# First weights loaded four pieces ahead, second weights split by VectorE and ScalarE, in an attention and two-MLP kernel

## The chip, the cores and the metric

The kernel runs on one core of one Trainium2 chip. The metric is the device time of one execution in microseconds. Before the change it is 1040.72 us, the median of 3 runs (1040.44 to 1042.83).

## What is computed

Three stages, each fed by the one before: a block-causal attention over 4 batches of 8 heads, 576 positions and 64 columns a head; an MLP with leaky ReLU; and a second MLP with a piecewise activation. The reference, cut:

```python
mask = (pos[:, None] // 64) >= (pos[None, :] // 64)
attn = softmax(np.where(mask, q @ k.T / np.sqrt(D), -1e9)) @ v     # per batch and head
x = attn.transpose(0, 2, 1, 3).reshape(2304, 512)
h = x @ w_in                       # 512 -> 2048, first MLP
x = np.maximum(0.01 * h, h) @ w_out
h = x @ w2_in                      # second MLP
g = np.where(h >= 1, h, np.where(h <= -1, 0.0, (h + 1) ** 2 / 4))
out = g @ w2_out
```

## The kernel before, in words

Products need more precision than one pass gives, so most operands are split into a high and a low part ("hi" and "lo", made by a copy and a subtraction) and three products are added up on TensorE (`three`, L536 to L539). The first batch's attention runs in plain float32 instead.

**Weights.** Both MLPs' weights come in as 64-bit words and lie in 16 slices f of 2 pieces each, 32 pieces an MLP, 512 KB a piece. `load_w1` (L127) issues the load of a piece on SyncE's queue. `convert_w1` makes float32 of it in four instructions: a scale on ScalarE or PoolE (L43, L47), then L113, L114 and L115 on VectorE. After the second piece of a slice, `split_w` makes hi and lo of its two halves: `w1i` for the up-projection and `w1o` for the down-projection. All these tiles share one pool of 33 slots. `w_to(n)` converts up to piece n, and `load_to` runs ahead of it by `WL` pieces; `WL` pieces are also loaded before anything else but the first two heads:

```python
loads_to(1)                            # L616, L617
load_to(C["WL"])
...
while nw < min(n, 2 * KF):             # w_to, L607 to L611
    load_to(nw + C["WL"])
    with behind(C["pW"]):
        convert_w1(nw)
    nw += 1
```

In the first batch's attention one piece is converted every seven items, up to twelve; the rest is converted in block 0 of the first MLP, two pieces for each f.

**Heads.** `load_head` issues queries (L236), keys (L237) and values (L251) of a head of the first batch, or L241, L247 and L255 of a later one. The tiles have two slots, so head 2 can be loaded when head 0's scores are done.

**Order.** Tokens of the first MLP come in 9 blocks of 256. Everything up to block 6 is traced and then put in order by a planner (`arrange`): it simulates the five engines with costs of its own, takes on each engine the earliest traced instruction that is ready by its model, and fixes each engine's order, SyncE's queue of transfers among them. An engine then runs in that order, and waits where an operand or a buffer is not there yet. A tile gets its slot only after the first user of the tile before it in the same pool has started, so the place of a load in the trace limits how early it can be issued. From block 6 on the planner has no part.

**Second weights.** In blocks 6 and 7 `stage_w2` converts them and writes them to DRAM (`wdram`), through three buffers (load L148, store L151). In block 8, as each f of the first weights is used up, `split_w2` loads a slice back (L155) and splits it with the same `split_w`:

```python
copy(nc, pick(he, 2 * f + u, ph), x[:, 0], w[:, u])
tt(nc, pick(le, 2 * f + u, ph), x[:, 1], w[:, u], f32(x)[:, 0], ALU.subtract)
```

Here u is 0 for `w2i` and 1 for `w2o`, and `pick` takes the letter at that place: D is VectorE, A ScalarE, P PoolE. A copy shows as L30 on ScalarE and L32 on VectorE; a subtraction is L38 on either VectorE or PoolE. In the same stretch VectorE makes gh (L32, for every second f) and gl (L38) of the first MLP.

**Second MLP.** 5 blocks, four of 512 tokens and one of 256. `up2` clamps (L718), squares on ScalarE (L719), takes the maximum (L720) and splits (L721, L722); `down2` adds up output tiles of 128 tokens, m = 0 to 3, copies each from PSUM by `copy(nc, pick("osE", m), osb, ot[m])` (L738) into one of three buffers, and stores it from ScalarE's queue (L739).

Of the kernel before, what the change touches and what calls it, by code (L numbers as in the profile page):

```python
# [14 lines left out]
ALU = mybir.AluOpType  # L15
AX = mybir.AxisListType

C = {'yx': 2, 'WARM': 7, 'DT': [0, 0, 1, 1], 'LAGD': 2, 'VLD': 4, 'WS': 1, 'RS': 2, 'zb': 2, 'dhE': 'PA', 'dlE': 'DD', 'wrE': 'SSSA', 'rdE': 'S', 'PR': '', 'pW': '', 'pS': '', 'p2': '', 'pL': '', 'pG': '', 'lkE': 'D', 'fE': 'A', 'stF': 'A', 'SPLIT': [0, 0, 0, 0], 'WIN': [[0.75, 1.86], [2, 3.86], [3.9, 5.86]], 'PF': [8, 0, 0, 0], 'VF': [8, 0, 0, 0], 'FL': 2, 'LD': 1, 'rcE': 'D', 'fold': 'D', 'evL': 'D', 'ptb': 1, 'PACE': 1, 'LAG0': 1, 'LAG': 3, 'VL0': 2, 'VL': 1, 'YL': 1, 'YL2': 3, 'gB': 2, 'ghB': 3, 'F32S': 6, 'F32V': 6, 'CS': 4, 'CR': 7, 'CN': 12, 'WAHEAD': 5, 'WL': 10, 'cE': 'APPP', 'addE': 'DP', 'hiE': 'AA', 'loE': 'DD', 'evH': 'AAD', 'xeE': 'A', 'norm': 'PPPPP', 'vhiE': 'D', 'vloE': 'P', 'ghE': 'DA', 'glE': 'DD', 'xhE': 'AAPP', 'xlE': 'PDDP', 'B1S': 0.5, 'FILL': 0.96, 'STR': 1.2, 'sc': 4, 'g': 3, 'gh': 3, 'klE': 'D', 'khE': 'P', 'stA': 'PP', 'stC': 'PA', 'yevE': 'DA', 'w2lo': 'DP', 'w2hi': 'DD', 'S0': 'att', 'T0': 'y', 'V0': 'h', 'natt': 5, 'evA': 'A', 'LY': 4, 'LYB': 4, 'yhE': 'AD', 'ylE': 'DD', 'osE': 'AA', 'qhE': 'D', 'sg': 3, 'TS': 1, 'norm_0': 'P', 'xlE_1': 'DPPP', 'evH_0': 'A', 'xhE_1': 'ADPA', 'norm_1': 'ADADA', 'fold_0': 'P', 'qhE_1': 'D', 'glE_0': 'DD', 'evA_1': 'AA', 'klE_2': 'P', 'klE_3': 'P', 'vloE_3': 'P', 'qhE_2': 'A', 'khE_2': 'P', 'vhiE_1': 'P', 'vloE_2': 'P', 'vloE_1': 'P', 'qhE_3': 'A', 'xlE_2': 'PDDP', 'xeE_2': 'AD', 'vhiE_3': 'A', 'norm_2': 'DADPA', 'xeE_1': 'DA', 'xhE_0': 'DDAA', 'xlE_0': 'PDPP', 'evH_1': 'A', 'evA_0': 'AA', 'fold_1': 'P', 'vloE_0': 'D', 'vhiE_0': 'D', 'khE_1': 'P', 'ghE_1': 'DD', 'fE_e': 'AP', 'hiE_e': 'AA', 'loE_e': 'DD', 'dlE_3': 'PD'}
P = 128
NEG = -1.0e30  # L20
EPS = 1.0e-9
# [29 lines left out]
def attention_moe_moe(ctx: ExitStack, tc: tile.TileContext, qkv, w1, w2, out, B, H, S, D):  # L51
# [22 lines left out]
    ps = [pctx.enter_context(tc.tile_pool(name="ps", bufs=1, space=bass.MemoryType.PSUM))]  # L74
    C["nh"] = 6 - C["natt"]
    nbanks = {"y": 2, "h": C["nh"], "att": C["natt"] - (2 if C["PR"] else 0)}

# [51 lines left out]
    def convert_w1(n):  # L129
        f, u = n // 2, n % 2  # L130
        ph = "e" if n < C["CN"] else ""
        if u == 0:
# [25 lines left out]
    def pick(n, i, ph=None):  # L158
        e = C.get(f"{n}_{ph}") or C.get(f"{n}_{str(ph)[:1]}") or C[n]
        return e[i % len(e)]  # L160
# [4 lines left out]
    two_p = mctx.enter_context(tc.tile_pool(name="two", bufs=2, side="right"))  # L165
    gpool = (two_p, C["g"], C["gh"])
    actx = ExitStack()
# [25 lines left out]

    passes = [(b, gs) for b in range(B) for gs in ([(0,), (1,)] if C["SPLIT"][b] else [(0, 1)])]
    due = [(b * S + GROUPS[gs[0]][0]) // NB for b, gs in passes]
# [812 lines left out]
```

## Time and profile before

| | |
|---|---|
| median of 3 runs | 1040.72 us |
| the profiled execution | 1038.87 us |
| its span, first to last instruction | 1037.1 us |
| TensorE busy | 1000.7 us, 96% |
| VectorE busy | 713.9 us, 69% |
| ScalarE busy | 470.7 us, 45% |
| PoolE busy | 224.8 us, 22% |
| mean granted clock of TensorE | 0.992 |

The rows in a later section come from that one execution. Times are microseconds from the start of its span; PE is TensorE, PEld its weight loads, DVE VectorE, ACT ScalarE, POOL PoolE (GpSimd), SP SyncE, which only issues transfers. A matmul in float32 leaves two records. Busy time is no limit by itself: an engine that waits costs time only where TensorE, the fullest engine, waits for it in the end.

### The profile page before, as it was taken

Reading aid. Unit: us, or ns where it says so; the run is one execution under the profiler, and the core shown is the slowest. Engines: PE = TensorE matmul, PEld = TensorE weight load, DVE = VectorE, ACT = ScalarE, POOL = GpSimd, SP = SyncE. Lnnn points to the kernel's source line nnn. Section 1 sums busy time; section 2 is a strip of 40 time slices with the busy share of each in tenths; the row PEclk is TensorE's granted clock in tenths of the full one; section 3 lists DMA queues with packets and bytes.
Section 4 is the critical chain, followed back from the end, with each engine's and each line's share of the span. In section 5 each row is a group of like instructions: output and inputs, shape, how many; then the busy total and the mean of one; then the engine's idle time right before and its main releaser. Section 6 shows DMA issues by size and latency. Waiting matters only on the chain. (4 is left out here: it accounts for less than half of the span.)

```text
span 1037.1 us, 16659 instructions
## 1 busy us (share of the span) xinstructions
PE 1000.7 (96%) x5518; PEld 847.1 (82%) x5518; DVE 713.9 (69%) x1850; ACT 470.7 (45%) x1167; POOL 224.8 (22%) x291
## 2 busy tenths in 40 slices
PE   8799999999989999999999999999999999999998
PEld 6557888888878888898988797888888888888897
DVE  7889999998898878877787798435334433433343
ACT  6678667675555644554443321223323322322233
POOL 4345022243333454644010144000000000000000
PEclk9999999999999999999999999999999999999999
DMA  9745023227778776774889884001100100000010
GB/s 352 262 152 178 22 51 77 59 64 150 150 139 182 156 150 145 142 169 99 276 298 282 250 273 121 1 1 41 41 1 1 62 1 1 36 5 1 1 41 21
DMA packets 194117, 115.39 MB, mean 111 GB/s; under 512 B 148208, under 2 KB 167152, under 8 KB 194032
## 3 DMA queue, kind: packets, MB, share of 16 engines
q1 hardware_dynamic: 165840, 106.47, 37.3%
q10 hardware_dynamic: 28192, 7.87, 3.2%
q8 instruction: 43, 0.70, 0.3%
q14 instruction: 42, 0.34, 0.1%
HBM read 83.62 MB, written 30.67 MB: 110 GB/s over the span
## 5 line engine op out<-in xcount | busy, mean ns | idle before, releaser
L537 PE MATMUL h<-xh,w1i 128*128 128x256 f32 x576 | 166.9, 290 | 5.8 <-ACT g L542 5.5
L538 PE MATMUL h<-xl,w1i 128*128 128x256 f32 x576 | 164.4, 286 | 1.2 <-DVE xl L38 0.9
L539 PE MATMUL h<-xh,w1i 128*128 128x256 f32 x576 | 164.1, 285 | 0.0
L719 ACT ACTIVATE sq<-cl,half 128x512 f32<-128x512 f32 (+1 forms) x80 | 54.4, 679 | 202.6 <-DVE cl L718 202.6
L718 DVE TENSOR_SCALAR cl<-hh 128x512 f32<-128x512 f32 (+1 forms) x80 | 51.0, 637 | 121.5 <-PE hh L539 121.4
L537 PEld LDWEIGHTS h<-xh,w1i 128*128 128x128 f32 x576 | 109.5, 190 | 15.4 <-ACT g L542 10.3
L567 PE MATMUL y<-w1o,gh 128*128 128x512 f32 x288 | 117.1, 407 | 2.4 <-DVE gh L32 2.1
L300 ACT ACTIVATE p<-s,nm 64x64 f32<-64x64 f32 (+2 forms) x192 | 91.1, 478 | 62.2 <-DVE nm L286 27.0
L537 PE MATMUL hh<-yh,w2i 128*128 128x512 f32 (+1 forms) x320 | 118.1, 369 | 0.3 <-DVE gg L720 0.3
L538 PE MATMUL hh<-yl,w2i 128*128 128x512 f32 (+1 forms) x320 | 118.0, 369 | 0.0
L539 PE MATMUL hh<-yh,w2i 128*128 128x512 f32 (+1 forms) x320 | 117.8, 368 | 0.0
L538 PEld LDWEIGHTS h<-xl,w1i 128*128 128x128 f32 x576 | 109.8, 191 | 5.8 <-DVE xl L38 1.9
L568 PE MATMUL y<-w1o,gh 128*128 128x512 f32 x288 | 114.2, 396 | 0.0
L734 PE MATMUL o<-w2o,ggl 128*128 128x512 f32 x288 | 114.0, 396 | 0.0
L735 PE MATMUL o<-w2o,ggh 128*128 128x512 f32 x288 | 113.9, 395 | 0.0
L539 PEld LDWEIGHTS h<-xh,w1i 128*128 128x128 f32 x576 | 109.8, 191 | 0.6
L570 PE MATMUL y<-w1o,gl 128*128 128x512 f32 x288 | 92.3, 399 | 2.3 <-DVE gl L38 2.2
L720 DVE TENSOR_TENSOR gg<-hh,sq 128x512 f32<-128x512 f32 (+1 forms) x80 | 51.0, 637 | 56.0 <-ACT sq L719 55.8
L286 DVE TENSOR_REDUCE nm<-s 128x1 f32<-128x288 f32 (+2 forms) x192 | 80.0, 424 | 9.3 <-PE s L277 5.6
L47 POOL TENSOR_SCALAR p<-p,rc 128x448 f32<-128x448 f32 (+4 forms) x88 | 60.6, 694 | 119.1 <-ACT p L300 34.9
L733 PE MATMUL o<-w2o,ggh 128*128 128x512 f32 x288 | 86.0, 396 | 0.0
L542 ACT ACTIVATE g<-h 128x256 f32<-128x256 f32 x144 | 54.2, 379 | 69.6 <-PE h L539 58.1
(110 smaller groups left out, 2059.4 us busy)
## 6 DMA issues: line engine op xcount, KB each, us to landing
wr<-in_w_dram SPq DMA_DIRECT2D x64, 512.0 KB, 5.4
wdram<-wt SPq DMA_DIRECT2D x32, 256.0 KB, 3.7
w<-wdram SPq DMA_DIRECT2D x16, 512.0 KB, 5.2
rq<-in_qkv_dram SPq DMA_DIRECT2D x24, 288.0 KB, 3.0
rk<-in_qkv_dram SPq DMA_DIRECT2D x24, 288.0 KB, 2.9
pT1l<-z SPq DMA_DIRECT2D x16, 384.0 KB, 3.9
ydram<-yx SPq DMA_DIRECT2D x72, 64.0 KB, 2.2
out_dram<-osb ACTq DMA_DIRECT2D x18, 256.0 KB, 2.9
```

What stands on the lines that cost most here:

```text
L47: return nc.gpsimd.tensor_scalar(out, in_, by, 1.0, op0=ALU.mult, op1=ALU.mult)
L286: mark["D"] = nc.vector.tensor_reduce(nm[:n, j:j + 1], s[:n, :kw], axis=AX.X, op=ALU.max, negate=True)
L300: mark["A"] = nc.scalar.activation(o, s, AF.Exp, bias=nm[:n, 0:1], scale=es, accum_out=sm[:n, j:j + 1])
L537: nc.tensor.matmul(ps_ap, wh, xh, start=first, stop=False)
L538: nc.tensor.matmul(ps_ap, wh, xl, start=False, stop=False)
L539: nc.tensor.matmul(ps_ap, wl, xh, start=False, stop=last)
L567: nc.tensor.matmul(yt[m], gh[:, ms], wh, start=f == 0, stop=False)
L568: nc.tensor.matmul(yt[m], gh[:, ms], wl, start=False, stop=False)
L570: nc.tensor.matmul(yt[m], gl[:, ms], wh, start=False, stop=f == KF - 1)
L733: nc.tensor.matmul(ot[m], gh[:, ms], wh, start=f == 0, stop=False)
L734: nc.tensor.matmul(ot[m], gl[:, ms], wh, start=False, stop=False)
L735: nc.tensor.matmul(ot[m], gh[:, ms], wl, start=False, stop=f == KF - 1)
```

## The change

Four entries of the table of settings `C` change. `WL` goes from 10 to 4: four pieces of the first weights are loaded at the start, and each later one is loaded four pieces ahead of the conversion in the trace. `w2hi` and `w2lo` give the engines that split the second weights: the high part of `w2i` moves from VectorE to ScalarE, and the low part of `w2o` from PoolE to VectorE; the high part of `w2o` and the low part of `w2i` stay on VectorE. `osE` moves the PSUM copies of output tiles with m = 1 and m = 3 from ScalarE to VectorE.

```diff
 C = {
...
-    'WL': 10,
+    'WL': 4,
...
-    'w2lo': 'DP', 'w2hi': 'DD',
+    'w2lo': 'DD', 'w2hi': 'AD',
...
-    'osE': 'AA',
+    'osE': 'AD',
...
 }
```

## Rows read from the trace of the kernel before

**Rows 1.** Busy time by stretch (us, instructions), granted clock, transfer share, GB/s.
```profile
core 0: us, PE busy (x) PEld busy (x) DVE busy (x) ACT busy (x) POOL busy (x), PEclk, DMA share, GB/s
0.00:95.70 95.70, 82.94 (x378) 56.27 (x378) 83.11 (x312) 69.75 (x207) 41.41 (x60) 0.96 0.67 235
95.70:142.00 46.30, 45.47 (x291) 40.59 (x292) 45.35 (x108) 30.13 (x69) 5.18 (x4) 1.00 0.20 66
142.00:490.00 348.00, 333.81 (x2165) 297.91 (x2164) 300.01 (x933) 205.46 (x594) 144.84 (x203) 0.99 0.59 126
614.60:632.70 18.10, 16.38 (x93) 13.75 (x92) 17.77 (x29) 2.79 (x7) 9.68 (x6) 1.00 0.68 228
```

**Rows 2.** The same view, shorter stretches of the first batch's attention.
```profile
19.00:36.50 17.50, 12.90 (x60) 8.18 (x60) 17.33 (x57) 11.48 (x34) 5.07 (x7) 1.00 1.00 371
40.00:45.00 5.00, 2.38 (x10) 1.56 (x11) 4.91 (x13) 3.04 (x10) 2.80 (x4) 0.99 0.67 224
45.00:50.00 5.00, 5.00 (x24) 3.83 (x22) 2.71 (x9) 2.50 (x6) 1.41 (x2) 0.67 0.37 103
60.00:65.00 5.00, 2.54 (x14) 1.60 (x13) 3.86 (x22) 2.50 (x7) 2.83 (x5) 1.00 0.95 333
65.00:70.00 5.00, 5.00 (x16) 2.35 (x15) 3.92 (x16) 4.39 (x15) 1.51 (x2) 0.66 0.52 199
```

**Rows 3.** TensorE's timeline: start, duration, instruction, in brackets the wait before it.
```profile
4.64 4.37 PE L277 MATMUL s<-kh,qs 128*64 128x64 f32 x12
...
26.48 2.63 PE L277 MATMUL s<-kh,qs 128*64 128x64 f32 x10
...
64.13 0.30 PE L277 MATMUL s<-kh,qs 128*64 128x64 f32 x2 [2.46 <-DMA kh<-in_qkv_dram]
```

**Rows 4.** Timeline of the transfer queue on SyncE: issues, not landings.
```profile
3.55 8.13 SPq L127 DMA_DIRECT2D wr<-in_w_dram  x10
12.80 0.33 SPq L236 DMA_DIRECT2D qs<-in_qkv_dram  x1
14.02 0.33 SPq L237 DMA_DIRECT2D kh<-in_qkv_dram  x1
```

**Rows 5.** Issue to landing, min/median/max: queries (0 to 95 us), first weights (to 140).
```profile
DMA to landing us min/median/max: 3.0/4.5/9.6
...
DMA to landing us min/median/max: 3.5/6.5/11.1
```

**Rows 6.** TensorE's timeline at the end of block 8 and the start of the second MLP.
```profile
628.94 0.50 PE L567 MATMUL y<-w1o,gh 128*128 128x512 f32 x1 [1.09 <-DVE gh L32]
...
632.17 0.73 PE L570 MATMUL y<-w1o,gl 128*128 128x512 f32 x2 [0.63 <-DVE gl L38]
...
644.10 0.50 PE L537 MATMUL hh<-yh,w2i 128*128 128x512 f32 x1 [0.30 <-DVE gg L720]
```

**Rows 7.** Timelines of VectorE and of PoolE in block 8.
```profile
605.13 0.29 DVE L32 CAST gh<-g 128x256 fp32r<-128x256 f32 x1
...
615.89 1.39 DVE L32 CAST gh<-g 128x256 fp32r<-128x256 f32 x1
...
615.51 1.62 POOL L38 TENSOR_TENSOR w2o<-w,w2o 128x512 fp32r<-128x512 f32 x1 [1.69 <-DVE w2o L32]
```

**Rows 8.** Groups of instructions: busy us, mean ns of one, idle time before.
```profile
L718 DVE TENSOR_SCALAR cl<-hh 128x512 f32<-128x512 f32 (+1 forms) x80 | 51.0, 637 | 121.5 <-PE hh L539 121.4
...
L38 DVE TENSOR_TENSOR w2i<-w,w2i 128x512 fp32r<-128x512 f32 x16 | 11.9, 747 | 0.0
...
L30 ACT ACTIVATE w1i<-w 128x512 fp32r<-128x512 f32 x16 | 10.1, 629 | 4.3 <-DVE w L115 4.3
...
L32 DVE CAST w2o<-w 128x512 fp32r<-128x512 f32 x16 | 6.7, 418 | 0.0
```

**Rows 9.** ScalarE's timeline at output copies: a block's fourth, and the last two.
```profile
819.38 0.60 ACT L30 ACTIVATE osb<-o 128x512 f32<-128x512 f32 x1 [2.70 <-DMA out_dram<-osb]
...
1032.85 1.09 ACT L30 ACTIVATE osb<-o 128x512 f32<-128x512 f32 x2 [1.75 <-PE o L735]
```

**Rows 10.** Waits, whole span: us in total, times, longest.
```profile
DVE wr L113 <- DMA wr<-in_w_dram: 12.1, 14, 1.9
```

**Rows 11.** Waits of the transfer queue on SyncE, 0 to 150 us.
```profile
SPq L251 <- PE v L424: 13.5, 2, 7.2
```

More of the change, by code (lines that the diff above doesn't have):

```diff
@@ L16 @@
 AX = mybir.AxisListType
-C = {'yx': 2, 'WARM': 7, 'DT': [0, 0, 1, 1], 'LAGD': 2, 'VLD': 4, 'WS': 1, 'RS': 2, 'zb': 2, 'dhE': 'PA', 'dlE': 'DD', 'wrE': 'SSSA', 'rdE': 'S', 'PR': '', 'pW': '', 'pS': '', 'p2': '', 'pL': '', 'pG': '', 'lkE': 'D', 'fE': 'A', 'stF': 'A', 'SPLIT': [0, 0, 0, 0], 'WIN': [[0.75, 1.86], [2, 3.86], [3.9, 5.86]], 'PF': [8, 0, 0, 0], 'VF': [8, 0, 0, 0], 'FL': 2, 'LD': 1, 'rcE': 'D', 'fold': 'D', 'evL': 'D', 'ptb': 1, 'PACE': 1, 'LAG0': 1, 'LAG': 3, 'VL0': 2, 'VL': 1, 'YL': 1, 'YL2': 3, 'gB': 2, 'ghB': 3, 'F32S': 6, 'F32V': 6, 'CS': 4, 'CR': 7, 'CN': 12, 'WAHEAD': 5, 'WL': 10, 'cE': 'APPP', 'addE': 'DP', 'hiE': 'AA', 'loE': 'DD', 'evH': 'AAD', 'xeE': 'A', 'norm': 'PPPPP', 'vhiE': 'D', 'vloE': 'P', 'ghE': 'DA', 'glE': 'DD', 'xhE': 'AAPP', 'xlE': 'PDDP', 'B1S': 0.5, 'FILL': 0.96, 'STR': 1.2, 'sc': 4, 'g': 3, 'gh': 3, 'klE': 'D', 'khE': 'P', 'stA': 'PP', 'stC': 'PA', 'yevE': 'DA', 'w2lo': 'DP', 'w2hi': 'DD', 'S0': 'att', 'T0': 'y', 'V0': 'h', 'natt': 5, 'evA': 'A', 'LY': 4, 'LYB': 4, 'yhE': 'AD', 'ylE': 'DD', 'osE': 'AA', 'qhE': 'D', 'sg': 3, 'TS': 1, 'norm_0': 'P', 'xlE_1': 'DPPP', 'evH_0': 'A', 'xhE_1': 'ADPA', 'norm_1': 'ADADA', 'fold_0': 'P', 'qhE_1': 'D', 'glE_0': 'DD', 'evA_1': 'AA', 'klE_2': 'P', 'klE_3': 'P', 'vloE_3': 'P', 'qhE_2': 'A', 'khE_2': 'P', 'vhiE_1': 'P', 'vloE_2': 'P', 'vloE_1': 'P', 'qhE_3': 'A', 'xlE_2': 'PDDP', 'xeE_2': 'AD', 'vhiE_3': 'A', 'norm_2': 'DADPA', 'xeE_1': 'DA', 'xhE_0': 'DDAA', 'xlE_0': 'PDPP', 'evH_1': 'A', 'evA_0': 'AA', 'fold_1': 'P', 'vloE_0': 'D', 'vhiE_0': 'D', 'khE_1': 'P', 'ghE_1': 'DD', 'fE_e': 'AP', 'hiE_e': 'AA', 'loE_e': 'DD', 'dlE_3': 'PD'}
@@ new lines @@
+C = {'yx': 2, 'WARM': 7, 'DT': [0, 0, 1, 1], 'LAGD': 2, 'VLD': 4, 'WS': 1, 'RS': 2, 'zb': 2, 'dhE': 'PA', 'dlE': 'DD', 'wrE': 'SSSA', 'rdE': 'S', 'PR': '', 'pW': '', 'pS': '', 'p2': '', 'pL': '', 'pG': '', 'lkE': 'D', 'fE': 'A', 'stF': 'A', 'SPLIT': [0, 0, 0, 0], 'WIN': [[0.75, 1.86], [2, 3.86], [3.9, 5.86]], 'PF': [8, 0, 0, 0], 'VF': [8, 0, 0, 0], 'FL': 2, 'LD': 1, 'rcE': 'D', 'fold': 'D', 'evL': 'D', 'ptb': 1, 'PACE': 1, 'LAG0': 1, 'LAG': 3, 'VL0': 2, 'VL': 1, 'YL': 1, 'YL2': 3, 'gB': 2, 'ghB': 3, 'F32S': 6, 'F32V': 6, 'CS': 4, 'CR': 7, 'CN': 12, 'WAHEAD': 5, 'WL': 4, 'cE': 'APPP', 'addE': 'DP', 'hiE': 'AA', 'loE': 'DD', 'evH': 'AAD', 'xeE': 'A', 'norm': 'PPPPP', 'vhiE': 'D', 'vloE': 'P', 'ghE': 'DA', 'glE': 'DD', 'xhE': 'AAPP', 'xlE': 'PDDP', 'B1S': 0.5, 'FILL': 0.96, 'STR': 1.2, 'sc': 4, 'g': 3, 'gh': 3, 'klE': 'D', 'khE': 'P', 'stA': 'PP', 'stC': 'PA', 'yevE': 'DA', 'w2lo': 'DD', 'w2hi': 'AD', 'S0': 'att', 'T0': 'y', 'V0': 'h', 'natt': 5, 'evA': 'A', 'LY': 4, 'LYB': 4, 'yhE': 'AD', 'ylE': 'DD', 'osE': 'AD', 'qhE': 'D', 'sg': 3, 'TS': 1, 'norm_0': 'P', 'xlE_1': 'DPPP', 'evH_0': 'A', 'xhE_1': 'ADPA', 'norm_1': 'ADADA', 'fold_0': 'P', 'qhE_1': 'D', 'glE_0': 'DD', 'evA_1': 'AA', 'klE_2': 'P', 'klE_3': 'P', 'vloE_3': 'P', 'qhE_2': 'A', 'khE_2': 'P', 'vhiE_1': 'P', 'vloE_2': 'P', 'vloE_1': 'P', 'qhE_3': 'A', 'xlE_2': 'PDDP', 'xeE_2': 'AD', 'vhiE_3': 'A', 'norm_2': 'DADPA', 'xeE_1': 'DA', 'xhE_0': 'DDAA', 'xlE_0': 'PDPP', 'evH_1': 'A', 'evA_0': 'AA', 'fold_1': 'P', 'vloE_0': 'D', 'vhiE_0': 'D', 'khE_1': 'P', 'ghE_1': 'DD', 'fE_e': 'AP', 'hiE_e': 'AA', 'loE_e': 'DD', 'dlE_3': 'PD'}
```

## The prediction

> **What bounds the kernel now.** I read the busy time by stage first, then fine windows where TensorE is not full, then the timelines of TensorE and of the transfer queue around those gaps. The four stretches of [rows 1] show a kernel that TensorE bounds nearly everywhere, with VectorE close behind. In the first 95.70 us, in which the first batch's eight heads run, TensorE is busy 82.94 us and VectorE 83.11 us: neither is full, so the stage is a chain of short waits between engines. In block 0 (95.70 to 142) both are full, 45.47 and 45.35 us of 46.30. From 142 to 490 us TensorE idles 348.00 - 333.81 = 14.2 us in all.
>
> Inside the first stage [rows 2] place the idle time. From 19.00 to 36.50 us TensorE idles 17.50 - 12.90 = 4.6 us while the transfer engines are full (share 1.00, 371 GB/s) and VectorE is busy 17.33 us. From 40 to 45 and from 60 to 65 us it idles 2.62 and 2.46 us. After each of these two the granted clock falls: 0.67 and 0.66 on average over the next 5 us, so part of each runs at 1.2 instead of 2.4 GHz, and loses about 0.33 x 5 = 1.7 us of full-speed time. [Rows 3] name two causes: the first scores of head 2 start only at 26.48 us, and the gap near 64 us ends with a key load (2.46 us).
>
> [Rows 4] say why head 2 is late. The transfer queue issues the ten pieces ahead in 8.13 us from 3.55 us on, so head 2's queries go out at 12.80 and its keys at 14.02 us. [Rows 5]: a query load lands after 3.0 us at best and 9.6 us at worst in this stage, so 12.80 + 9.6 = 22.4 us.
>
> The other place is the end of block 8. Between 614.60 and 632.70 us VectorE is busy 17.77 of 18.10 us and TensorE 16.38 [rows 1]; the waits that end last there are 1.09 us for gh and 0.63 us for gl, and later 0.30 us for gg [rows 6], 2.0 us together, all on VectorE.
>
> **The change part by part.**
>
> *Six pieces fewer at the start.* Six loads of 512 KB leave the head of the queue: 3.15 MB at 371 GB/s [rows 2] are 8.5 us of full transfer engines. Every later piece moves too: all 28 pieces after the first four are now issued some three conversions before their own, behind loads of heads (L236, L237, L251, and L241, L247, L255 for the second batch) that they used to pass. Nothing is added in number. The queries of head 2 need only head 0's scores out of the way, which are over at 4.64 + 4.37 = 9.0 us [rows 3]; so an issue near 9 us and a landing 4.5 us later, the median of [rows 5], gives 14 us in place of 22.4. What that frees on TensorE is at most the 4.6 us of idle time from 19.00 to 36.50 us. VectorE is full there (17.33 of 17.50 us), partly with conversions that fill its time and can slide into later idle, so I take half: 2.3 us. Bounds: 4.6 + 2.46 + 1.7 = 8.8 us if the gap at 64 us and the drop of clock behind it go too, and a loss by late pieces, priced among the rivals. I do not take the key stall itself: in the middle of the stage one piece is loaded per piece converted, before as after, so the same transfers share the engines there. Block 0 covers conversions that slide: VectorE's total to 142 us is 128.5 of 142 us, and TensorE, busy 45.47 of 46.30 us in block 0 [rows 1], hardly waits for the conversions there. If that cover is gone, each further us of conversion is a us of TensorE.
>
> *Second weights without PoolE.* For each f VectorE loses one cast (0.418 us), which ScalarE takes over at the 0.629 us of the same copy of the first weights, and gains the second subtraction, at most the 0.747 us of the one it does already [rows 8]: +0.33 us. But [rows 7] show a gh cast of 128x256 that takes 0.29 us alone and 1.39 us while PoolE's subtraction of 1.62 us runs: 1.10 us lost per PoolE subtraction. Six of these lie in the stretch to 632.70 us (PoolE x6 in [rows 1]), so VectorE falls by 6 x (1.10 - 0.33) = 4.6 us, from 17.77 to 13.2 us, under TensorE's 16.38. ScalarE goes from 2.79 to 2.79 + 6 x 0.63 = 6.6 us of 18.10. The waits of [rows 6] then have no cause: I take all 2.0 us. Bounds: 0 to -2.0, and +0.63 us if one ScalarE copy that waits for its transfer holds the activation behind it at a bad moment. What is late next there is TensorE itself, or the transfer of the last two second-weight pieces.
>
> *Output copies.* Every second copy of an output tile goes from ScalarE to VectorE. [Rows 9]: at block ends the fourth copy waited 2.70 us for a free buffer and held ScalarE's queue; now it holds VectorE's, with clamp, maximum and subtraction behind it. TensorE had no idle time there, and the total wait moves, not grows: 0, covered by the two tiles in flight; without that cover it would be up to 2.7 us at each of four block ends. At the very end two copies take 1.09 us on ScalarE; the second, on VectorE, costs about the 0.637 us of a 128x512 read of PSUM [rows 8] instead of some 0.55, so +0.1 us on the path.
>
> *Sum.* -2.3 - 2.0 + 0.1 = -4.2 us. The profiled execution took 1038.87 us, 1.77 above its span, and gives 1034.7; it lies 1.85 us under the median of the runs, 1040.72, which gives **1036.5 us**. About 0.3% (3.1 us) is what a measurement of this kernel can tell from no change.
>
> **The rivals.**
>
> *The early loads were hidden anyway.* For it: VectorE is full from 19.00 to 36.50 us, so earlier scores only queue for its maxima, and block 0 is full on both engines, so what is won is given back. Against: TensorE's idle time and the full transfer engines coincide. Then only the second weights pay: -2.0 + 0.1, 1038.8 us.
>
> *The pieces come too late (slower).* The place is VectorE's queue in the first stage and block 0: a conversion (L113) whose piece has not landed holds the maxima and reciprocals behind it, for which ScalarE, PoolE and then TensorE wait. The nearest row is the staging of the second weights, which loads just ahead of use: VectorE waited 12.1 us for 32 pieces [rows 10], 0.38 us each, and 28 pieces make 10.6 us. Speaking for it: pieces landed after 6.5 us in the median and 11.1 at worst [rows 5], and the transfer queue itself stands still for up to 7.2 us before a head's values [rows 11], with a piece then behind it. Against: VectorE idles 12.6 us in the first stage, so some of this is covered. Half on the path and one more drop of clock, 5.3 + 1.7 - 1.9 = +5.1: 1045.8 us. It decides once a piece lands later than the conversions of the three pieces ahead of it last. The Trainium skill, DMA: Bandwidth & Descriptors, section Rules for kernel authors, says to issue a transfer early and wait for it late; by that rule this case is the likely one. The trace of before bears it out only for the staging, and shows its price at the start, the late heads.
>
> *The new order falls badly.* The planner orders everything up to block 6 anew from the changed trace, so the 14.2 us of idle time from 142 to 490 us are dealt again. A quarter more, with one clock drop more, is 3.5 + 1.7 - 1.9 = +3.3: 1044.0 us; it can as well give something back. That the change does not do what it says I leave out: the letters name the engines outright.
>
> **How the numbers follow.** Forecast 0.45, all of it faster; hidden anyway 0.27, all within 0.3%; a bad order 0.12, of which 0.03 within; late pieces 0.16. So faster 0.45, same 0.30, slower 0.25. The forecast's own range runs from -8.8 - 2.0 + 0.1 = -10.7 (1030.0) to 1037.6, the edge of what can be told. The range for 8 in 10 goes on to the late pieces at 1045.8 above and a little beyond the lower bound: 1029 to 1046.
>
> **What would show it.** Right: head 2's queries issued near 9 us; its scores well before 26 us; less idle time from 19 to 36 us; the first up-projection before 95.7 us; no wait of VectorE for a piece; gh casts near 0.29 us around 615 us and no TensorE wait for gh or gl before the second MLP. Wrong: VectorE waiting at L113 in the first 130 us; TensorE waiting for w1i in block 0; more clock drops than the two of the first stage; the wait for gg growing. If the first 142 us take as long as before, the first term fails; if the second MLP begins its work with the same lag, the second does.

## The result, and the profile after

The changed kernel takes 1027.70 us (median of 4 runs, 1026.92 to 1028.11) where the kernel before took 1040.58 beside it (4 runs): a ratio of 0.9886 with a 95% interval of 0.9863 to 0.9909, some 12 us faster. The forecast had 4.2 us, and the lower end of its range, 1029, lies above the result.

The page of the changed kernel, its span and its busiest engines:

```profile
span 1025.1 us, 16641 instructions
...
PE 995.7 (97%) x5518; PEld 844.8 (82%) x5518; DVE 709.0 (69%) x1859; ACT 473.1 (46%) x1174; POOL 195.8 (19%) x275
```

The span fell from 1037.1 to 1025.1 us. Where, is read from one instruction in both traces, the first up-projection matmul of each block: where it starts earlier than before, time has been won up to there.

| start of | before | after | won so far |
|---|---|---|---|
| block 0 of the first MLP | 95.7 | 84.0 | 11.7 |
| block 3 | 295.4 | 285.8 | 9.6 |
| block 7 | 533.8 | 525.5 | 8.3 |
| block 8 | 581.1 | 571.9 | 9.2 |
| second MLP | 632.7 | 621.3 | 11.4 |
| its second block | 716.3 | 704.3 | 12.0 |
| end of the span | 1037.1 | 1025.1 | 12.0 |

So the first stage wins 11.7 us, blocks 0 to 6 give 3.4 of it back, and block 7, block 8 and the second MLP's first block win 0.9, 2.2 and 0.6 us. From the second MLP's second block on nothing changes.

Busy time of the changed kernel by stretch, with the columns of [rows 1]; the first row is its first stage, the next four lie inside it, the last two are block 8 and the first block of the second MLP:

```profile
core 0: us, PE busy (x) PEld busy (x) DVE busy (x) ACT busy (x) POOL busy (x), PEclk, DMA share, GB/s
0.00:84.00 84.00, 78.16 (x378) 55.02 (x379) 76.39 (x303) 65.10 (x201) 41.18 (x60) 0.98 0.64 217
...
19.00:36.50 17.50, 16.29 (x81) 10.73 (x79) 16.85 (x72) 13.80 (x41) 8.08 (x12) 1.00 0.68 239
40.00:45.00 5.00, 4.31 (x22) 2.67 (x22) 4.86 (x16) 3.79 (x12) 3.05 (x5) 1.00 0.39 127
60.00:65.00 5.00, 5.00 (x26) 3.50 (x25) 4.90 (x21) 4.28 (x16) 3.74 (x5) 1.00 0.20 80
...
75.00:80.00 5.00, 3.48 (x21) 2.52 (x19) 4.91 (x24) 4.52 (x15) 2.17 (x3) 1.00 0.30 92
...
571.90:621.30 49.40, 48.33 (x299) 42.90 (x298) 40.19 (x87) 20.14 (x45) 1.85 (x3) 1.00 0.75 244
621.30:704.30 83.00, 83.00 (x361) 67.66 (x360) 39.69 (x63) 23.07 (x35) 0.00 (x0) 1.00 0.09 20
```

Against [rows 2], TensorE's idle time falls in every one of the three gaps of before: from 4.6 to 1.2 us in 19 to 36.5, from 2.62 to 0.69 in 40 to 45, from 2.46 to 0 in 60 to 65, 7.8 us together (the same times hold later work in the changed kernel, so this is a rough comparison); a new gap of 1.5 us from 75 to 80 gives part of it back. Over the whole stage idle time fell from 95.70 - 82.94 = 12.8 to 5.8 us. The same 378 matmuls also count 4.8 us less busy time; one drop of the clock fewer (0.96 to 0.98 in the stage's mean) is 1.7 of these, and for the rest no row gives a cause.

TensorE's timeline of the changed kernel: the first scores of head 2 and of head 4, which were at 26.48 [rows 3] and at 47.95 us.

```profile
19.51 1.39 PE L277 MATMUL s<-kh,qs 128*64 128x64 f32 x6
...
34.65 1.39 PE L277 MATMUL s<-kh,qs 128*64 128x64 f32 x6
```

Its transfer queue, against [rows 4]: four pieces in front, then head 2's queries and keys at once; the last row is head 4's keys.

```profile
3.55 2.21 SPq L127 DMA_DIRECT2D wr<-in_w_dram  x4
...
8.28 0.33 SPq L236 DMA_DIRECT2D qs<-in_qkv_dram  x1
8.65 0.43 SPq L237 DMA_DIRECT2D kh<-in_qkv_dram  x1
...
27.71 0.42 SPq L237 DMA_DIRECT2D kh<-in_qkv_dram  x1
```

Head 2 is what the forecast spoke of: queries issued near 9 us, scores well before 26. Head 4 is what it did not. In the kernel before, head 4's keys were there long before anything used them. Their issue, their time to landing (26 to 40 us), and TensorE's first matmul with them, all of the kernel before:

```profile
30.90 0.43 SPq L237 DMA_DIRECT2D kh<-in_qkv_dram  x1
...
DMA to landing us min/median/max: 3.7/3.9/4.2
...
47.95 1.00 PE L277 MATMUL s<-kh,qs 128*64 128x64 f32 x4
```

Landed at latest at 30.90 + 4.2 = 35.1 us (its queries at 34.4), used at 47.95: a wait of 12.9 us with no transfer in it, and in its last part lies the idle time from 40 to 45 us. There TensorE stands at transposes of earlier heads, which wait for ScalarE's copies; in its order head 4's scores come behind them. TensorE's timeline of the kernel before:

```profile
41.05 0.63 PE L374 MATMUL t<-ident,p 64*64 64x64 f32 x3 [1.13 <-ACT pT1h L30]
43.25 0.30 PE L374 MATMUL t<-ident,p 128*128 128x128 f32 x1 [1.57 <-ACT pT0h L30]
```

In the changed kernel the same keys land near 31.7 and are used at 34.65. What follows from a late head 4 is a late head 6, which is loaded into head 4's slots. Head 4's last scores end at 56.6 us before and at 44.7 us after, and head 6's queries and keys are issued just behind them, first before, then after the change:

```profile
56.63 1.75 SPq L236 DMA_DIRECT2D qs<-in_qkv_dram  x1
58.43 0.42 SPq L237 DMA_DIRECT2D kh<-in_qkv_dram  x1
```

```profile
44.69 0.33 SPq L236 DMA_DIRECT2D qs<-in_qkv_dram  x1
45.06 0.43 SPq L237 DMA_DIRECT2D kh<-in_qkv_dram  x1
```

The keys issued at 58.43 us are those that TensorE waits 2.46 us for at 64.13 [rows 3]. Issued 13.4 us earlier, they cause no wait.

At the other end, block 8 and the second MLP's first block as they were, with the same columns, for the last two rows above:

```profile
581.10:632.70 51.60, 48.81 (x298) 42.74 (x297) 46.50 (x84) 13.27 (x32) 21.82 (x14) 1.00 0.72 233
632.70:716.30 83.60, 83.30 (x362) 67.56 (x360) 41.01 (x66) 21.28 (x32) 7.11 (x5) 1.00 0.09 20
```

PoolE is all but gone from both stretches (21.82 to 1.85 and 7.11 to 0), VectorE has 6.3 us less to do in block 8 though it makes more instructions, and the two together take 132.4 us instead of 135.2. Of these 2.8 us, 2.0 are TensorE's idle time, which falls from 3.1 to 1.1 us; the other 0.8 is busy time of the same matmuls, for which no row gives a cause. VectorE's line for gh there (compare [rows 7]), and the one group of TensorE's waits from 571 to 650 us that is left of [rows 6] and its like:

```profile
607.14 0.28 DVE L32 CAST gh<-g 128x256 fp32r<-128x256 f32 x1
```

```profile
PE h L538 <- DVE xl L38: 0.9, 2, 0.6
```

The waits for gh, gl and gg are gone; the one for xl was there before, with the same 0.9 us.

### The profile page after: what moved, and what is told of

Read it like the earlier page. It is cut to its first block, busy times and chain, and to the rows that moved or that the text cites. A ratio compares the mean times of both kernels' runs of the same rounds, so it can differ in the third digit from the quotient of the medians.

```text
span 1025.1 us, 16641 instructions
## 1 busy us (share of the span) xinstructions
PE 995.7 (97%) x5518; PEld 844.8 (82%) x5518; DVE 709.0 (69%) x1859; ACT 473.1 (46%) x1174; POOL 195.8 (19%) x275
## 5 line engine op out<-in xcount | busy, mean ns | idle before, releaser
L722 DVE TENSOR_TENSOR ggl<-gg,ggh 128x512 fp32r<-128x512 f32 (+1 forms) x80 | 51.1, 638 | 46.7 <-ACT ggh L721 46.2
```

## Experiments

Fifteen kernels in four rounds, each compared with runs of the kernel before on the same chip (medians 1039.15, 1039.04, 1038.97 and 1038.37 us). Four explanations of the first stage were open. **A**: the ten transfers in front make heads 2 and 3 really late. **B**: pieces loaded early let conversions run early, and these take VectorE from the heads. **D**, formed after the first round: the planner charges every transfer a price, takes ten pieces ahead for a long backlog, believes the keys of heads 2 and 4 late, and puts other work ahead of them on each engine, whether they are late or not. (The price is in the planner's code; the times that it believed were not printed, so its belief is inferred.) And that the order simply fell well, without a cause that can be named. For the second weights the rival to PoolE in VectorE's way was the copy moved to ScalarE by itself.

All that follows can be read beside this table. Each time is from the profiled execution, one for each kernel: the start of block 0, the start of block 7, and the time from block 8 to the second MLP's second block (135.2 before, 132.4 after; differences of times rounded to 0.1 us).

| kernel | block 0 at | block 7 at | block 8 and next | ratio, 95% |
|---|---|---|---|---|
| before | 95.7 | 533.8 | 135.2 | 1 |
| changed | 84.0 | 525.5 | 132.4 | 0.9886 [0.9863, 0.9909] |
| e1 | 83.9 | 527.5 | 136.5 | 0.9935 [0.9913, 0.9957] |
| e2 | 92.8 | 533.5 | 131.5 | 0.9980 [0.9963, 0.9997] |
| e3 | 86.4 | 530.6 | 135.0 | 0.9916 [0.9897, 0.9936] |
| e4 | 87.0 | 524.2 | 138.7 | 0.9978 [0.9962, 0.9994] |
| e5 | 86.8 | 534.8 | 137.0 | 1.0013 [0.9990, 1.0036] |
| e6 | 84.8 | 534.9 | 134.3 | 0.9993 [0.9971, 1.0016] |
| e7 | 92.5 | 534.7 | 134.9 | one run |
| e8 | 94.2 | 535.2 | 131.8 | one run |
| e9 | 93.4 | 536.7 | 132.6 | 1.0022 [1.0002, 1.0042] |
| e10 | 87.3 | 533.9 | 131.5 | 0.9963 [0.9944, 0.9982] |
| e11 | 88.6 | 530.8 | 132.3 | 0.9918 [0.9880, 0.9956] |
| e12 | 88.4 | 527.2 | 134.3 | 0.9909 [0.9879, 0.9939] |
| e13 | 87.3 | 532.6 | 135.0 | 0.9988 [0.9967, 1.0009] |
| e14 | 85.6 | 525.7 | 134.0 | 0.9929 [0.9902, 0.9955] |
| e15 | 88.1 | 528.4 | 132.1 | 0.9905 [0.9871, 0.9938] |

### The two halves, each alone

```diff
-    'WL': 10,                        # e1
+    'WL': 4,
```

> Only the lead of the first weights goes from ten pieces to four; second weights and output copies stay as before. In the changed kernel the first up-projection started at 84.0 us instead of 95.7, block 8 ended 2.2 us shorter and the whole 12.0 us shorter. If the two edits add up, the lead alone gives the 11.7 us at the start, loses some 2 to 3 us again in blocks 0 to 7 as the changed kernel did, and the end of block 8 stays as it was: about 1040.6 - 9.2 = 1031.4 us, first up-projection near 84 us. If the gain comes from the second weights, it stays within 2 us of the kernel before.

```diff
-    'w2lo': 'DP', 'w2hi': 'DD', 'osE': 'AA',      # e2
+    'w2lo': 'DD', 'w2hi': 'AD', 'osE': 'AD',
```

> Only the second weights' engines and the output copies change; ten pieces ahead as before. The planner's part is the same, so the trace up to block 6 should repeat, first up-projection at 95.7 us and five drops of the clock. If the waits of 2.0 us on VectorE near 629 to 644 us go, the whole is 2 to 3 us shorter, 1038 us; if they were replaced by others, no change.

The loads alone take 1031.96 us and make the whole of the first stage's gain (83.9 against 84.0). The split alone takes 1037.2 us; it leaves the order up to block 6 as it was and keeps a gain only from block 8 on. Its first stage takes 92.8 us all the same, 2.9 less than in the kernel before: so far apart can two profiles of one order lie. By the ratios the two are worth 0.65% and 0.20%, 0.85% together, and both at once 1.14%. The missing 3 us is partly scatter: e1 has the order of the changed kernel up to block 6, and yet reaches block 7 2.0 us later in its profile, at a granted clock of 0.98 from block 0 to block 7 where the changed kernel had 0.99.

### Real lateness or the order

Both next kernels take the reasons apart. e3 keeps the burst of ten in front and only then goes on with a lead of four; e4 begins with four and lets the lead grow to ten after the fifth piece.

```diff
-    load_to(C["WL"])                 # e3, with 'WL': 4
+    load_to(10)
```

> Ten pieces are loaded at the start as before, but each later one only four ahead, so none is loaded until the sixth conversion. Theory A (the ten transfers at the head of the queue make heads 2 and 3 late): the first up-projection stays near 95 us and the gain is lost, about 1038 to 1041 us. Theory B (a long lead lets the planner put conversions early on VectorE, in front of the softmax): conversions run ahead only by the ten, and the stage shortens by half or more, 84 to 90 us. Theory C (the planner's order happened to fall well): anywhere, with no relation to when heads 2 and 3 land.

```diff
-            load_to(nw + C["WL"])    # e4
+            load_to(nw + (4 if nw < 5 else 10))
...
-    load_to(C["WL"])
+    load_to(4)
```

> Four pieces at the start as in the changed kernel, lead four up to the fifth conversion, then ten, so the six other pieces come in a burst after heads 2 and 3. Theory A: heads 2 and 3 land near 17 and 20 us as in the changed kernel and the first up-projection starts at 84 to 88 us. Theory B: conversions run ahead again from the fifth on, and the stage is back near 92 to 96 us. Theory C: anywhere.

e3 is the sharper of the two. TensorE's first scores of head 2 and of head 4 in e3, and the time to landing of the keys of heads 2 and 3 (issued at 13.51 and 16.64 us):

```profile
26.66 4.07 PE L277 MATMUL s<-kh,qs 128*64 128x64 f32 x14
...
36.13 0.85 PE L277 MATMUL s<-kh,qs 128*64 128x64 f32 x4
```

```profile
DMA to landing us min/median/max: 9.4/9.7/10.0
```

The burst is real, and its effect too: keys land near 23.5 us, and head 2 starts at 26.66 us, as late as before. But the stage ends at 86.4 us, 9.3 earlier than before and only 2.5 later than e1. e15 below, with the same order up to block 6, ends it at 88.1, 4.1 later than the changed kernel. So A is worth an estimated 2.5 to 4.1 us of the 11.7, and head 4, at 36.13 instead of 47.95 us, holds most of the rest. e4 has the heads early and ends its first stage at 87.0; it kept 9.6 us up to block 7, more than the changed kernel, and then lost 3.5 in block 8 and the next, with PoolE in them.

The 86.4 us of e3 lie where B had been expected to put it, the 87.0 of e4 do not. B is in part true of the early stage: by 30 us VectorE had begun 8 first-weight conversions in the kernel before, 6 in the changed one, in e1 and in e4, 7 in e3; by 70 us it was 14 in all five. But it is not what decides: e9 below has begun only 5 by 30 us, and its first stage is as long as before.

### The planner's price of a transfer

The planner books a transfer's share of the transfer engines at 3.3 ns per KB. [Rows 2] show 371 GB/s with the engines full, 1024 / 371 = 2.8 ns per KB. e5 changes that number alone and leaves ten pieces ahead; e6 does the same to the changed kernel; e9 makes transfers dearer in the changed kernel. None of these numbers adds a byte or an instruction: only the order is written anew, that of SyncE's queue of transfers with the others.

```diff
-        ..., kb * (7.6 if small else 6 if spread else 3.3)
+        ..., kb * (7.6 if small else 6 if spread else 2.6)   # e5 on before, e6 on the changed kernel
+        ..., kb * (7.6 if small else 6 if spread else 4.5)   # e9 on the changed kernel
```

> The kernel before, ten pieces ahead; only the planner's own price of a transfer is lower (2.6 instead of 3.3 ns per KB in the sum that stands for the shared transfer engines, near what the 371 GB/s of the trace give). No transfer, engine or lead is changed, only the orders that the planner writes. Theory D (the order is written for a backlog of transfers that is longer than the real one, so the scores of heads 2 and 4 stand behind other work on TensorE although their keys have landed): head 4's scores start well before the 47.9 us of before, and the first up-projection near 86 to 90 us. Theory A (the real transfers are late): head 4 as before, stage 92 to 96 us, perhaps with TensorE waiting for keys. Theory C (luck of the order): anywhere from 84 to 98.

> The changed kernel with the same lower price of a transfer in the planner. Theory D: four pieces ahead leave little backlog to misjudge, so less is gained than from the same edit on the kernel before: the first up-projection between 82 and 85 us, the whole within 4 us of the changed kernel (1024 to 1030 us). If orders now run ahead of real landings, TensorE or VectorE waits for transfers and it is slower by some us.

> The changed kernel, four pieces ahead, with a higher price of a transfer in the planner (4.5 instead of 3.3 ns per KB); the loads, engines and leads stay those of the changed kernel. Theory D: the planner again believes in a backlog that is not there, so scores of heads 2 and 4 stand later than the 19.5 and 34.6 us of the changed kernel though their keys land about as before, and the first up-projection moves from 84.0 to 88 us or more. Theory A (real transfers alone decide): first stage within 1 us of 84.

TensorE's timeline in e5, head 2 and head 4:

```profile
23.34 0.30 PE L277 MATMUL s<-kh,qs 128*64 128x64 f32 x2 [1.32 <-DMA kh<-in_qkv_dram]
...
37.25 0.33 PE L277 MATMUL s<-kh,qs 128*64 128x64 f32 x2
```

With ten pieces still in front, head 2's keys are as late as ever, but TensorE now stands waiting for them (1.32 us) and starts the moment they land. Head 4's keys, issued at 30.90 us as before, are used at 37.25 instead of 47.95. Block 0 starts at 86.8 us: 8.9 us won with the ten pieces still in front. Later loads follow from the new order: head 6's keys go out at 45.01 us instead of 58.43, behind head 4's earlier scores. Against the mean of the four kernels whose order up to there is that of before (before, e2, e7, e8: 95.7, 92.8, 92.5 and 94.2, mean 93.8) the gain is 7.0.

And the other way round, e9, the changed kernel with dearer transfers: issue, time to landing (26 to 40 us) and first use of head 4's keys.

```profile
28.35 0.42 SPq L237 DMA_DIRECT2D kh<-in_qkv_dram  x1
...
DMA to landing us min/median/max: 3.0/3.1/3.1
...
44.93 0.48 PE L277 MATMUL s<-kh,qs 128*64 128x64 f32 x2
```

The keys are there at 31.5 us and lie unused for 13.5 us, as in the kernel before. Block 0 starts at 93.4 us. So the price alone moves the first stage by 7 to 9 us in both directions, through the order, and D is shown for the first stage. What the real transfers add is then about the difference between e5 and the changed kernel, 2.8 us, beside the 2.5 to 4.1 of e3 and e15; single profiles do not say it more closely.

For the whole time D is not enough. e5 and e6 arrive at block 7 1.0 and 1.1 us later than before: all that the first stage had won is lost in blocks 0 to 6. The whole of e6 is 1039.68 us, where 1024 to 1030 had been expected. I put that down to the price, which also orders the later transfers, and tried it for the first heads' loads and the first weights only.

```diff
-  6 if spread else 3.3
+  6 if spread else 2.6 if outs[0][0].name.startswith(("qs", "kh", "vv", "wr")) else 3.3
```

> The kernel before, ten pieces ahead; the planner's lower price (2.6 instead of 3.3 ns per KB) holds for the first batch's queries, keys, values and the first weights alone, all later transfers keep the old one. The first stage should repeat that of the run with the price lowered everywhere (86.8 us). That run gave its 8.9 us back by block 7. If the lower price of the later batches' transfers spoiled the order there, most of the gain is now kept: block 7 starts 4 to 9 us earlier than before and the whole is 1031 to 1036 us. If an earlier start as such is worn away in blocks 0 to 6, because something other than TensorE sets their pace, it is given back again: 1037 to 1041 us.

> The same lower price for the first batch and the first weights, on the changed kernel. With the price lowered everywhere it lost 14 us from the first up-projection to block 7 against the kernel before. If the later transfers' price did that, it now ends near the changed kernel, 1024 to 1030 us; if not, near 1039 us.

With a lead of four that holds: e14 reaches block 7 8.1 us early where e6 was 1.1 late, so the price of the other transfers had spoilt the later order. (What e6 lost from block 0 to block 7 is 12.0 us by the table, not the 14 of the expectation; e14 takes 1032.64 us, above the expected 1030.) With ten ahead it does not: e13 wins 8.4 us and has 1.2 left at block 7. It loses them early (8.4 at block 0, 6.4 at block 1, 3.8 at block 2, 1.8 at block 3), and e5, which has the same order up to 247 us in block 2, loses there alike (8.9, 7.0 and 4.5). Why an order with ten ahead loses its lead there, and the changed kernel only 2.1 in the same blocks, the runs do not settle.

### How far ahead

```diff
-    'WL': 4,
+    'WL': 3,                         # e10, the changed kernel otherwise
+    'WL': 6,                         # e11, the changed kernel otherwise
```

> The changed kernel with three pieces ahead. If fewer pieces at the start are what counts, the first stage is as short as with four (83 to 85 us) and the whole 1026 to 1031 us. If pieces now come too late, VectorE waits at L113 for them and the stage and block 0 grow by several us.

> The changed kernel with six pieces ahead, between the two. If the backlog of transfers sets the first stage, it lies between four ahead (84.0 us) and ten ahead (92.8 to 95.7 us): 85 to 89 us, and the whole about 1028 to 1034 us. If four was a lucky order, no such place between is kept.

Three, four, six and ten ahead give a first stage of 87.3, 84.0, 88.6 and 92.5 to 95.7 us. From four up the stage grows with the lead, as far as single profiles show it; a lead of three is no better, and e10 takes 1036.23 us where 1026 to 1031 had been expected for a short first stage. Late pieces are not the reason: in e10's first 130 us VectorE waited for a piece once,

```profile
DVE wr L113 <- DMA wr<-in_w_dram: 1.9, 1, 1.9
```

and in the changed kernel not at all. e10 lost another 6.8 us in blocks 0 and 1 of the first MLP (8.4 ahead at block 0, 1.6 at block 2), to an order I cannot explain either.

### The second weights, part by part

```diff
-    'w2hi': 'DD',                    # e7, PoolE kept
+    'w2hi': 'AD',
```

> The kernel before with the high part of w2i on ScalarE; the low part of w2o stays on PoolE, output copies as before. VectorE loses 0.42 us per f but still meets PoolE's subtractions. If the collision with PoolE makes the waits at the end of block 8, block 8 keeps most of its 51.6 us (51 or more) and gh casts keep reaching 1.39 us; if it is VectorE's plain load, block 8 falls to 49.5 or less.

```diff
-    'w2lo': 'DP',                    # e8, no copy moved
+    'w2lo': 'DD',
```

> The kernel before with the low part of w2o on VectorE and nothing on ScalarE or elsewhere changed: VectorE carries the whole split, 0.3 us more per f than in the changed kernel plus the cast, but PoolE is silent. If the collision makes the waits, block 8 falls to about 49 us as in the run with all of the split changed (48.5 us); if the plain load does, it stays at 51 us or grows.

Block 8 and the second MLP's first block in e7 (first pair) and in e8 (second pair), with the columns of [rows 1]:

```profile
583.20:632.80 49.60, 48.56 (x299) 42.78 (x298) 43.80 (x73) 20.29 (x45) 20.87 (x15) 1.00 0.70 227
632.80:718.10 85.30, 83.59 (x362) 67.42 (x361) 41.11 (x61) 23.05 (x35) 7.25 (x5) 1.00 0.10 25
```

```profile
582.50:631.30 48.80, 48.12 (x299) 42.91 (x298) 42.42 (x97) 13.35 (x32) 1.01 (x2) 1.00 0.75 244
631.30:714.30 83.00, 83.00 (x362) 67.59 (x361) 41.08 (x69) 21.39 (x32) 0.00 (x0) 1.00 0.08 20
```

Taking PoolE out (e8) brings the two stretches to 131.8 us, as the whole split does (131.5 in e2). Relieving VectorE of a copy and leaving PoolE in (e7) brings 134.9, next to nothing, although VectorE makes 73 instructions in block 8 there, 84 before and 97 in e8. By block 8 alone e7 is no clear case: 49.6 us, where 51 or more was expected for the collision and 49.5 or less for VectorE's load. What block 8 won came back in the next block, as a wait that was 0.30 us before [rows 6]:

```profile
PE hh L537 <- DVE gg L720: 1.7, 1, 1.7
```

VectorE's subtraction tells why: for w2i in e7, with PoolE's for w2o behind it, and then for w2i in e8 (ns, min/median/max, first and last start):

```profile
L38 DVE TENSOR_TENSOR w2i<-w,w2i x16: 677/686/1772, 589.8 to 649.5; 128x512 fp32r<-128x512 f32 x16
...
L38 POOL TENSOR_TENSOR w2o<-w,w2o x16: 1283/1614/3097, 590.9 to 649.1; 128x512 fp32r<-128x512 f32 x16
```

```profile
L38 DVE TENSOR_TENSOR w2i<-w,w2i x16: 650/684/686, 588.6 to 646.2; 128x512 fp32r<-128x512 f32 x16
```

The median is the same, the longest is not: 1772 ns where PoolE is at work, 686 without it. Over the table, the seven kernels with PoolE in the split have 134.9 to 138.7 us in that column (mean 136.0), and the ten without have 131.5 to 134.3 (mean 132.7): the two sets do not overlap, and the split is worth 3.3 us. TensorE's waits part them too: in block 8 it waits for gl in all seven with PoolE and for gh in all but e7, and in none of the ten without; e4, e5, e6, e12 and e14 also wait 1.1 to 1.5 us there for yx (L575), with and without PoolE. The copies of output tiles cost nothing that shows: from the start of the second MLP to the end of the span it is 404.3 us before, 403.8 in e8, where they stayed on ScalarE, and 403.8 in e2 and in the changed kernel.

### Looking for something better

e4 had kept the most up to block 7 and e3 had the best median with the old split, so both ways of loading were run with the new split.

```diff
-            load_to(nw + C["WL"])    # e12: the changed kernel with e4's loads
+            load_to(nw + (4 if nw < 5 else 10))
...
-    load_to(C["WL"])                 # e15: the changed kernel with e3's burst
+    load_to(10)
```

> Four pieces at the start and ten ahead from the sixth conversion on, now with the changed split of the second weights and output copies. In the run without the split the first batch ended at 87.0 us and block 6 began 10.2 us earlier than before, more than the 8.5 of the changed kernel, and the end lost by VectorE's collision with PoolE. If the split is worth its 3 to 4 us here too, the whole is 1027 to 1034 us, at best as fast as the changed kernel.

> Ten pieces at the start, four ahead later, with the changed split. Without the split this was 1030.3 us, with the first stage at 86.4 us. With 3 to 4 us of the split: 1026 to 1029 us, as fast as the changed kernel, although heads 2 and 3 land as late as before; slower than 1031 us if the changed kernel's short start burst is needed.

They take 1031.07 and 1031.50 us. e12 is e4 with the new split, and 6.2 us faster than it by the medians, more than the split is worth elsewhere; e15 does not beat e3 in its median (1030.28), though its last stretch is 2.9 us shorter, and lies above the 1026 to 1029 expected. The changed kernel, at 1027.70, stays the fastest of all.

## Why the prediction was wrong

**The failed step is the first term, 2.3 us, which measured 11.7** between the two traces (9.8 against the mean of the four kernels with the order of before). It said: "What that frees on TensorE is at most the 4.6 us of idle time from 19.00 to 36.50 us", and of the later stall, "I do not take the key stall itself: in the middle of the stage one piece is loaded per piece converted, before as after". That reasons about transfers and takes the order of the engines as given. The order is an output of the loads: the planner writes it from its own idea of when they land. I used that for blocks 0 to 6, in the rival of the bad order, and not for the first stage, where it decided. e5 and e9 show it: 7 to 9 us come from the order. The rest, an estimated 2.5 to 4.1 us, is for transfers that were late in truth; this is the part that the 2.3 stood for. One step of it was off as well: head 2's queries were to land at 14 us, 4.5 us after their issue, and landed at 16.7, 8.4 us after it.

The key stall at 64 us was not set by the pieces beside it, as the sum had it. They may have slowed the load, which took 5.6 us there and 3.3 in the changed kernel; but head 6's keys were issued 13.4 us later, because head 4's scores, which held their slot, ran late. With head 4 early the stall is gone, in the changed kernel and in e5.

The row that should have led there was in the trace of before, and I read past it: head 4's keys had landed 12.9 us before their first matmul. The gap from 40 to 45 us was in [rows 2], and I put no cause to it; with a landed operand and idle TensorE in the same stretch, only the order or another engine's queue is left. The bound of 8.8 us was too small for the same reason: besides the 4.6 it held the gap of 2.46 us and one drop of the clock, but not the 2.62 us of 40 to 45.

**The second weights: right mechanism, and the right size for the waits.** The term was 2.0 us, the waits of [rows 6], and TensorE's idle time fell by 2.0 us. Measured over the two stretches are 2.8 us between the two traces, 3.7 for e2 and 3.3 over the table. That lifting PoolE's hold on VectorE does it is shown by e8, and by the waits that part the two sets of kernels; e7 alone would not decide. What the sum did not have is TensorE's busy time in these two stretches: 132.1 to 132.3 us in the kernels with PoolE in the split, 131.1 to 131.6 in those without. Its cause stays open. VectorE's work in the last 18.10 us before the second MLP fell to 14.8 us, where 13.2 was forecast.

**Output copies**: 0.1 us of loss predicted, none found.

**The rivals.** That the early loads were hidden anyway falls with e1, whose first stage is 11.8 us shorter. Late pieces: no wait of VectorE for a piece in the first 130 us, one of 1.9 us at a lead of three. The Trainium skill, DMA: Bandwidth & Descriptors, section Rules for kernel authors, says to issue early and wait late; with four pieces ahead the trace agrees, as VectorE waits for none of them in the first 130 us, and it does not show that earlier still is better: a longer lead paid nothing, and the transfers in front cost the heads' loads an estimated 2.5 to 4.1 us. The bad order is there in part: of 11.7 us won, 8.3 are left at block 7, and TensorE's idle time in blocks 0 to 6 rose from 15.5 to 18.2 us. That is close to the 3.5 us I had priced for it; it came on top of a much larger gain.

**The signs named ahead** came out: queries at 8.28 us, scores at 19.51, less idle time to 36 us, block 0 before 95.7, no wait for a piece, gh at 0.28 us, no wait for gh, gl or gg, and one clock drop in the first stage instead of two.

**Still open**: why orders with ten pieces ahead lose their lead in blocks 0 to 3, and so how much of the final 12 us is owed to a favourable order there. What is known is that the four kernels that share the order of before (before, e2, e7, e8) differ by 3.2 us at block 0 and by 1.3 at block 3, which suggests that part of an early lead is absorbed by these blocks in any case.

## What to carry to other kernels

Where an order is planned ahead, a change to loads changes the order of everything, and the prediction has to ask first what the planner believes and where it is wrong. The sign to look for is an operand that landed long before its first use while the consuming engine has idle time: no faster transfer mends that, but a price nearer to the measured one, or loads that the planner takes for cheaper, can. In this kernel that mended the first stage; the whole time followed only where the later order was kept as well. And when one engine is freed of another's interference, measure the whole stretch in which both work: the waits alone gave 2.0 of the 2.8 us here.

## What the runs showed of the hardware

PoolE's two-input subtraction held up VectorE even in a cast with one input: 1.39 us instead of 0.29, starting 0.38 us into PoolE's 1.62 us and ending 0.15 us after it [rows 7]. The other two slow casts of that trace, 1.35 and 1.39 us, end 0.15 us after a PoolE subtraction as well. That is a stop until PoolE is done, not a sharing. Where VectorE was at work first, PoolE waited: its subtraction at 608.96 us, begun beside a VectorE subtraction with more VectorE work right behind, took 3.4 us, and the gh cast at 610.95 us beside it only 0.29. VectorE's clamp, which reads PSUM, was not held up: 0.68 us beside PoolE's subtraction at 643.96 us, 0.69 in the median after 660 us, where PoolE is silent. The Trainium skill, SBUF — State Buffer, section Who interferes with whom, says that a cast in a two-port mode and GpSimd exclude each other for a whole instruction, with the first to start winning; the trace agrees. ScalarE's copies did not suffer: those for w2i have a median of 632 ns in e7 and in the changed kernel alike.

TensorE's clock fell in different places in executions with the same order: at 44.9, 65.4, 304.3, 369.1 and 430.6 us in the kernel before, at 34.0, 44.3 and 225.2 us in e2, each time to 1.2 GHz. The drops at 44.9 and 65.4 us follow the gaps of 2.62 and 2.46 us in TensorE's work [rows 2]. At an estimated 1.7 us for each, a profile with two drops more is 3.4 us longer with no difference in the program. The 72 runs of the kernel before in the four rounds ranged from 1034.5 to 1046.1 us: the 11 with a mean granted clock under 0.990 took 1041.6 us on average, the 16 at 0.994 or more 1038.2. Differences of 2 us between single profiles, in the table above too, carry nothing by themselves.
